# A spatial gate that leaves PSUM in its first two vector operations, with its product and its low half on GpSimd

## The chip, the cores and the metric

The kernel runs on one core of a Trainium2 chip. The metric is the device time of one execution in microseconds (us), as the median of several runs. The core has a matrix engine (PE, TensorE, with its weight loads shown apart as PEld), a vector engine (DVE, VectorE), a scalar engine (ACT, ScalarE), GpSimd (POOL) and a queue engine that issues transfers (SP). PE writes its results to PSUM; everything else lies in SBUF.

## The reference, cut to what matters

The model is a decayed linear attention, a feed-forward block and a gated block, for 4 batches of 768 tokens with 384 features. The change touches the two last lines of the gated block alone.

```python
def _moe2_ref(x, w_in, g_ln, w_sg, b_sg, w_out):
    h = gelu_tanh(x @ w_in)                       # 384 -> 1024
    u, v = h[..., :512], h[..., 512:]
    v_n = layer_norm(v) * g_ln
    v_s = np.einsum('ts,bsd->btd', w_sg, v_n) + b_sg[None, :, None]   # over the 768 tokens
    gated = u * v_s
    return x + gated @ w_out
```

## The kernel before

The tokens are cut into 24 chunks of 128 (4 batches of 6). A chunk's attention needs DMA transposes, two scans on VectorE, and small matmuls (`sc` L436, `psd` L518, `psy` L544 and L551), and it ends in an rms scale that GpSimd works out in a chain of small operations (L241 to L246). Its result `x` then goes through the feed-forward block, two chunks at a time: `pg` L633 is the first product, evicted by ScalarE (hT, L638) and VectorE (hT, L639); L667 is the second. The gated block makes `vg` from `pgv` (L707) and the factor u, called `uT`, from `pgu` (L732). Every fp32 operand of a matmul is split into two half-precision parts, a high part (a copy to f16) and a low part (the value less that copy), and each product is three matmuls. The helper `low` (L150) makes low parts, on VectorE or GpSimd.

The **spatial gate** is `D_units` (L740 to L769). It runs once per batch, when all six chunks of the batch have their `vn`. It has six units, one for each of three blocks of 256 tokens (`th`) and two halves of the features (`dp`). One unit is 36 matmuls of 128x256 into one PSUM tile `pgs`, two VectorE operations (scale by g, add b; L759), a VectorE product with u (L762), a ScalarE copy to the high part (L763), the low part (L150 through `low`) and a ScalarE square with a running sum for a range check (L766, tile `junk`, sum into `st_g`). `KG_` is 0, so `in_psum` is always true: all of these work in place in the PSUM tile `pgs`, and the low part is made on VectorE. The last reader of the tile is L766. The high and low parts overwrite the memory of `uT` (the tile `gt` is the same bytes), and so they are called `uT` in the traces. `E_units` then makes `pgo` (L781) from them, adds x on VectorE (L783), and writes the output by DMA.

PSUM tiles with tag "g" have three buffers, and `pg`, `pg2`, `pgv`, `pgu`, `pgs` and `pgo` take turns in them. PE can start a unit when the tile three units earlier has lost its last reader.

The order of the work is not written out engine by engine. Each attention step and each unit gets a due time from a table of constants (L920 to L974, `events`), the list is sorted by it, and a scheduler sets each engine's instructions in a row by its own timeline. Each engine takes its instructions in that order, and one that waits holds those behind it. The attention of later batches runs among the units of earlier ones, up to the third gate. The fourth gate has no attention beside it.

At the end of `split_path` eleven range checks (L977 to L998) are made, each of three small VectorE operations through a tile `ok` in the pool `p1` (one buffer, tag "tm"), then two more (L1000, L1001), a GpSimd all-reduce (L1002) and a cast (L1003). The program reads the flag before it ends.

Of the kernel before, what the change touches and what calls it, by code (L numbers as in the profile page):

```python
# [7 lines left out]
F32 = mybir.dt.float32  # L8
# [5 lines left out]
ALU = mybir.AluOpType  # L14
# [3 lines left out]
P = 128  # L18
EPS = 1e-6
LATE, TC, D0, DS, DX, KQ, NE, KA, LD, S0, A0, S1, A1, S2, A2, S3, A3, S4, A4, S5, A5, C0, R0, C1, R1, C2, R2, C3, R3, MB, MD, QB, HB, KV, KG_, KW, KW2 = 16.42, 19.13, 24, 0.88, 1.18, 8.0, 4.0, 8.0, 5.66, 0.8, 16, 13, 12, 28, 14, 38, 14, 46, 14, 54, 14, 2, 3, 18, 3, 36, 3, 60, 5, 224.0, 96.0, 0.0, 96.0, 19.0, 0.0, 10.0, 0.0  # L20
# [19 lines left out]
def kernel(tc, q, k, v, alpha, g1, w1, w2, w_in, g2, w_sg, b_sg, w_out, out):  # L40
    nc = tc.nc
    with ExitStack() as ctx:
        keep = ctx.enter_context(tc.tile_pool(name="keep", bufs=1))
        ident = keep.tile([P, P], F32, name="ident")
        bad = keep.tile([1, 1], I32, name="bad")
        with ExitStack() as fast:
            split_path(fast, tc, ident, bad, q, k, v, alpha, g1, w1, w2, w_in, g2, w_sg, b_sg, w_out, out)
        flag = nc.values_load(bad[0:1, 0:1], min_val=0, max_val=1)
        with tc.If(flag > 0):
            with ExitStack() as slow:  # L50
                general_path(slow, tc, ident, q, k, v, alpha, g1, w1, w2, w_in, g2, w_sg, b_sg, w_out, out)


def split_path(ctx, tc, ident, bad, q, k, v, alpha, g1, w1, w2, w_in, g2, w_sg, b_sg, w_out, out):


    nc = tc.nc
# [11 lines left out]
    U = 256  # L69
# [8 lines left out]
    p1 = ctx.enter_context(tc.tile_pool(name="p1", bufs=1))  # L78
    p2 = ctx.enter_context(tc.tile_pool(name="p2", bufs=2))
# [31 lines left out]
    def junk():  # L111
        return p2.tile([P, 512], BF16, tag="cv", name="junk")
# [36 lines left out]
    def low(on_dve, out, in0, in1):  # L149
        (nc.vector if on_dve else nc.gpsimd).tensor_tensor(out=out, in0=in0, in1=in1, op=ALU.subtract)  # L150
# [464 lines left out]
    hT, x2T, uf, uT, vn, gt = {}, {}, {}, {}, {}, {}  # L615
# [124 lines left out]
    def D_units(b):  # L740
        units = []
        for th in range(S // U):
            for dp in range(KG // 2):
                def unit(th=th, dp=dp):
                    key = (b, th)

                    gt[key] = uf[key].bitcast(F16).rearrange("p (g a f t) -> p g a f t", g=KG // 2, a=2, f=2)
                    pg = ps.tile([P, 2, U], F32, tag="g", bufs=3, name="pgs")
                    for f in range(2):
                        d = 2 * dp + f  # L750
                        for n_, (s, a, r) in enumerate([(s, a, r) for s in range(NCH) for a, r in passes]):
                            nc.tensor.matmul(out=pg[:, f, :], lhsT=vn[b * NCH + s][:, a, d * P:(d + 1) * P],  # L752
                                             rhs=wgs[th][:, r, s, :], start=(n_ == 0),
                                             stop=(n_ == 3 * NCH - 1))
                    in_psum = b >= KG_
                    tm = pg if in_psum else p1.tile([P, 2, U], F32, tag="tm", name="tm")
                    for f in range(2):
                        d = 2 * dp + f
                        nc.vector.scalar_tensor_tensor(out=tm[:, f, :], in0=pg[:, f, :], scalar=g2c[:, d:d + 1],  # L759
                                                       in1=bbc[:, th * U:(th + 1) * U], op0=ALU.mult, op1=ALU.add)  # L760
                    o = slice(2 * dp, 2 * dp + 2)
                    nc.vector.tensor_tensor(out=tm, in0=tm, in1=uT[key][:, o, :], op=ALU.mult)  # L762
                    nc.scalar.activation(out=gt[key][:, dp, 0], in_=tm, func=AF.Copy)  # L763
                    low(in_psum, gt[key][:, dp, 1], tm, gt[key][:, dp, 0])
                    n_ = b * 6 + 2 * th + dp
                    nc.scalar.activation(out=junk()[:, 0:512].rearrange("p (a b) -> p a b", a=2), in_=tm,  # L766
                                         func=AF.Square, accum_out=st_g[:, n_:n_ + 1])
                units.append((unit, 36 * U / 2400.0, NW[3]))
        return units  # L769
# [48 lines left out]
    if True:  # L818
# [2 lines left out]
            nc.gpsimd.memset(t[:, 3, :, D:64], 1.0)  # L821
        nc.vector.memset(one, 1.0)

        cols = p1.tile([P, 2 * U], F32, tag="tm", name="cols")[:, 0:P]
        ones = p2.tile([P, DG], F32, tag="vg", name="ones")[0:1, 0:P]
        nc.vector.memset(ones, 1.0)
        unit = one.to_broadcast([P, P])
# [103 lines left out]
        for j in range(NG):  # L931
            b, c, n = groups[j]
# [57 lines left out]
        verdict = big.tile([P, len(checks) + 2], F32, name="verdict")  # L990
        fails, worst, allbad = verdict[:, 2:], verdict[:, 0:1], verdict[:, 1:2]
        for n, (src, lo, hi, shape) in enumerate(checks):
            ok = p1.tile([P, 2 * U], F32, tag="tm", name="ok")
            ok = ok[:, 0:shape[0]] if len(shape) == 1 else \
                ok[:, 0:shape[0] * shape[1]].rearrange("p (a b) -> p a b", b=shape[1])
            nc.vector.tensor_scalar(out=ok, in0=src, scalar1=lo, scalar2=None, op0=ALU.is_ge)
            nc.vector.scalar_tensor_tensor(out=ok, in0=src, scalar=hi, in1=ok, op0=ALU.is_le, op1=ALU.mult)
            nc.vector.tensor_reduce(out=fails[:, n:n + 1], in_=ok, op=ALU.min,  # L998
                                    axis=AX.XY if len(shape) == 2 else AX.X)
# [242 lines left out]
```

## Time and profile before

| What | Value |
|---|---|
| median of 3 runs | 701.03 us (700.08 to 703.02) |
| the profiled execution, its own time | 702.77 us |
| span of its trace | 701.0 us |
| mean granted TensorE clock | 0.992 of full speed |
| PE busy | 650.6 us (93%) |
| DVE busy | 465.3 us (66%) |
| ACT busy | 435.5 us (62%) |
| POOL busy | 181.0 us (26%) |

The profiled execution lies 1.74 us above the median, and 1.77 us of its time lie outside the span. PE is busy for all but 50.4 us. The gates run in about 223 to 251 us (batch 0), 382 to 407 us (batch 1), 541 to 569 us (batch 2) and 660 to 683.5 us (batch 3). Shares of the whole span say little here: the other engines are far from full on average and full in places.

### The profile page before, as it was taken

What the parts mean: (1) busy time and instruction counts of PE and PEld (TensorE: products, weight loads), DVE (VectorE), ACT (ScalarE), POOL (GpSimd) and SP (SyncE); (2) the same over time, 40 slices, a digit from 0 to 9 for tenths busy, and PEclk for the clock granted to TensorE, in tenths of its full rate; (3) what the DMA queues carried; (4) which work ended last, traced back from release to release, by engine and by line L of the source; (5) the groups of instructions that cost most, each with busy time, mean ns of one, the idle gap of its engine ahead of it and who ended that gap; (6) DMA issues with size and microseconds to landing.
All of it is one profiled execution on the core that took longest, in us unless ns stands there. A gap on an engine that the chain in (4) does not pass through costs nothing.

```text
span 701.0 us, 14486 instructions
## 1 busy us (share of the span) xinstructions
PE 650.6 (93%) x5658; PEld 489.4 (70%) x5658; DVE 465.3 (66%) x911; ACT 435.5 (62%) x871; POOL 181.0 (26%) x413
## 2 busy tenths in 40 slices
PE   5889998979999988989999978998989989999996
PEld 3757776767776875667777866676656877676783
DVE  7999675867476795557745896559655678333464
ACT  5887646676878488488755688488652656322230
POOL 2121101423516220433532220432404311201100
PEclk9999999999999999999999999999999999999999
DMA  9996679765475149367382159275140612110102
GB/s 227 226 260 167 204 178 169 155 113 95 91 121 80 28 86 190 84 108 116 59 115 56 30 100 183 76 127 85 40 86 15 88 34 58 34 24 12 36 1 72
DMA packets 228637, 70.64 MB, mean 101 GB/s; under 512 B 219472, under 2 KB 222544, under 8 KB 228560
## 3 DMA queue, kind: packets, MB, share of 16 engines
q1 hardware_dynamic: 228560, 69.63, 52.0%
q8 instruction: 46, 0.75, 0.5%
q14 instruction: 31, 0.25, 0.1%
HBM read 35.79 MB, written 4.72 MB: 58 GB/s over the span
## 4 chain that ended last, share of the span: by engine, by line
PE 43%; DVE 17%; ACT 17%; DMA 13%; issue 5%; POOL 3%; SPq 1%; ACTq 0%; DVEq 0%; POOLq 0%
PE pg L667 13%; PE pg L633 9%; PE pgs L752 6%; DMA stage<-stage 4%; PE pgu L732 4%; PE pgv L707 4%; PE pgo L781 3%; ACT stage L306 3%; DMA wgs<-wsp 2%; ACT junk L500 2%; ACT stage L290 2%; DMA inp<-in_alpha_dram 2%; DVE F L345 2%; DVE sc L449 2%; DMA inp<-in_q_dram 2%
## 5 line engine op out<-in xcount | busy, mean ns | idle before, releaser
L633 PE MATMUL pg<-xhT,w1s 128*128 128x256 f16 (+1 forms) x1404 | 151.5, 267 | 13.2 <-DVE hT L639 6.1
L633 PEld LDWEIGHTS <-w1s 128*128 128x128 f16 x1404 | 128.4, 99 | 31.2 <-issue 14.9
L667 PE MATMUL pg<-w2s,hT 128*128 128x384 f16 x864 | 143.7, 326 | 0.3 <-ACT vg L710 0.3
L667 PEld LDWEIGHTS <-hT 128*128 128x128 f16 x864 | 83.9, 98 | 54.3 <-issue 0.2
L752 PE MATMUL pgs<-wgs,vn 128*128 128x256 f16 x864 | 96.1, 273 | 1.5 <-ACT junk L766 1.5
L752 PEld LDWEIGHTS <-vn 128*128 128x128 f16 x864 | 84.0, 98 | 12.0 <-issue 1.7
L639 DVE SCALAR_TENSOR_TENSOR hT<-pg,hT 128x512 f16<-128x512 f32 (+1 forms) x74 | 49.3, 672 | 46.8 <-ACT hT L638 46.6
L306 ACT ACTIVATE stage<-stage 128x1024 uint16<-128x1024 uint16 x48 | 64.7, 1354 | 19.1 <-DMA stage<-stage 19.0
L290 ACT ACTIVATE stage<-inp 128x1024 uint16<-128x1024 uint16 x48 | 50.1, 1053 | 30.3 <-DVE K L345 18.4
L150 POOL TENSOR_TENSOR kh<-K,kh 128x512 f16<-128x512 f32 x17 | 20.4, 1199 | 129.2 <-ACT kh L414 129.2
L732 PE MATMUL pgu<-x2T,wis 128*128 128x256 f16 x432 | 50.7, 274 | 1.6 <-DVE hT L639 1.3
L707 PE MATMUL pgv<-wis,x2T 128*128 128x512 f16 x216 | 49.9, 381 | 1.5 <-DVE hT L639 1.2
L781 PE MATMUL pgo<-wos,uT 128*128 128x384 f16 x288 | 48.3, 326 | 1.2 <-DVE x L783 1.2
L732 PEld LDWEIGHTS <-wis 128*128 128x128 f16 x432 | 41.7, 98 | 9.1 <-DVE hT L639 2.2
L638 ACT ACTIVATE hT<-pg 128x512 f16<-128x512 f32 (+1 forms) x74 | 42.0, 577 | 9.7 <-PE pg L633 9.6
L500 ACT ACTIVATE junk<-inp 128x384 bf16<-128x384 f32 x72 | 37.2, 519 | 8.0 <-DMA inp<-in_q_dram 4.0
L781 PEld LDWEIGHTS <-uT 128*128 128x128 f16 x288 | 28.0, 98 | 19.9 <-issue 2.0
L150 POOL TENSOR_TENSOR qs<-F,qs 128x512 f16<-128x512 f32 x18 | 20.6, 1143 | 79.7 <-ACT qs L386 79.7
L707 PEld LDWEIGHTS <-x2T 128*128 128x128 f16 x216 | 20.9, 99 | 24.4 <-issue 2.1
L468 ACT ACTIVATE ss<-sc 128x512 f16<-128x512 f32 x36 | 21.1, 596 | 19.0 <-DVE sc L449 19.0
L759 DVE SCALAR_TENSOR_TENSOR pgs<-pgs,g2c,bbc 128x256 f32<-128x256 f32 x48 | 23.4, 487 | 11.3 <-PE pgs L752 10.6
L716 DVE TENSOR_SCALAR vg<-vg,mvv,rv 128x512 f32<-128x512 f32 x24 | 13.8, 579 | 24.4 <-POOL rv L246 23.9
(172 smaller groups left out, 1100.8 us busy)
## 6 DMA issues: line engine op xcount, KB each, us to landing
stage<-in_moe_w_ch_dram SPq DMA_DIRECT2D x24, 384.0 KB, 5.2
inp<-in_alpha_dram SPq DMA_DIRECT2D x24, 192.0 KB, 3.3
inp<-in_q_dram SPq DMA_DIRECT2D x24, 192.0 KB, 4.1
inp<-in_k_dram SPq DMA_DIRECT2D x24, 192.0 KB, 4.4
inp<-in_v_dram SPq DMA_DIRECT2D x24, 192.0 KB, 4.4
out_dram<-x SPq DMA_DIRECT2D x24, 192.0 KB, 2.4
stage<-in_moe_w_in_dram SPq DMA_DIRECT2D x4, 768.0 KB, 4.3
stage<-in_moe_w_sg_dram SPq DMA_DIRECT2D x6, 384.0 KB, 3.4
```

The source lines that it names most:

```text
L150: (nc.vector if on_dve else nc.gpsimd).tensor_tensor(out=out, in0=in0, in1=in1, op=ALU.subtract)
L290: nc.scalar.activation(out=sp, in_=t[:, n].rearrange("p h d -> p (h d)").bitcast(U16) .rearrange("p (x w) -> p w x", w=2), func=AF.Copy)
L306: nc.scalar.activation(out=words[:, :, :, gap:], in_=tr, func=AF.Copy)
L500: nc.scalar.activation(out=junk()[:, 0:DM].rearrange("p (h d) -> p h d", h=H), in_=t[:, n, :, 0:D], func=AF.Square, accum_out=st_in[:, i, ...
L633: nc.tensor.matmul(out=pg[:, f, :], lhsT=w1s[:, a, kk, ff * P:(ff + 1) * P], rhs=xhT[j][:, r, kk, o], start=(n_ == 0), stop=(n_ == 3 * KD ...
L638: nc.scalar.activation(out=hi, in_=src, func=AF.Relu)
L639: last_dve[0] = nc.vector.scalar_tensor_tensor(out=lo, in0=src, scalar=0.0, in1=hi, op0=ALU.max, op1=ALU.subtract)
L667: nc.tensor.matmul(out=box[s], lhsT=hidden(a, f, s), rhs=w2s[:, r, f, :], start=(f == 0 and a == 0 and r == 0), stop=(f == KF - 1 and r == 1))
L707: nc.tensor.matmul(out=pg, lhsT=x2T[j][:, a, kk, o], rhs=wis[:, r, kk, DG:DI], start=(n_ == 0), stop=(n_ == 3 * KD - 1))
L732: nc.tensor.matmul(out=pg[:, f, :], lhsT=wis[:, a, kk, ff * P:(ff + 1) * P], rhs=x2T[j][:, r, kk, 0:N], start=(n_ == 0), stop=(n_ == 3 * K ...
L752: nc.tensor.matmul(out=pg[:, f, :], lhsT=vn[b * NCH + s][:, a, d * P:(d + 1) * P], rhs=wgs[th][:, r, s, :], start=(n_ == 0), stop=(n_ == 3 ...
L781: nc.tensor.matmul(out=pg, lhsT=gt[key][:, d // 2, a, d % 2, o], rhs=wos[:, r, d, :], start=(d == 0 and a == 0 and r == 0), stop=(d == KG ...
```

## The change

The gate's first two VectorE operations now write to a new SBUF tile `tm` (pool `p2`, two buffers) instead of back to PSUM. The product with u reads and writes `tm`, and it runs on GpSimd. The low part runs on GpSimd too. ScalarE's copy and square read `tm`. The scratch tiles `cols` (in the prologue) and `ok` (the range checks at the end) move from `p1` to `p2` with the same tag "tm", so that they take turns in the two buffers of the gate's `tm`. Line numbers after the gate fall by one.

```diff
-                    in_psum = b >= KG_
-                    tm = pg if in_psum else p1.tile([P, 2, U], F32, tag="tm", name="tm")
+                    tm = p2.tile([P, 2, U], F32, tag="tm", name="tm")
                     for f in range(2):
                         d = 2 * dp + f
                         nc.vector.scalar_tensor_tensor(out=tm[:, f, :], in0=pg[:, f, :], scalar=g2c[:, d:d + 1],
                                                        in1=bbc[:, th * U:(th + 1) * U], op0=ALU.mult, op1=ALU.add)
                     o = slice(2 * dp, 2 * dp + 2)
-                    nc.vector.tensor_tensor(out=tm, in0=tm, in1=uT[key][:, o, :], op=ALU.mult)
+                    nc.gpsimd.tensor_tensor(out=tm, in0=tm, in1=uT[key][:, o, :], op=ALU.mult)
                     nc.scalar.activation(out=gt[key][:, dp, 0], in_=tm, func=AF.Copy)
-                    low(in_psum, gt[key][:, dp, 1], tm, gt[key][:, dp, 0])
+                    nc.gpsimd.tensor_tensor(out=gt[key][:, dp, 1], in0=tm, in1=gt[key][:, dp, 0], op=ALU.subtract)
...
-        cols = p1.tile([P, 2 * U], F32, tag="tm", name="cols")[:, 0:P]
+        cols = p2.tile([P, 2 * U], F32, tag="tm", name="cols")[:, 0:P]
...
-            ok = p1.tile([P, 2 * U], F32, tag="tm", name="ok")
+            ok = p2.tile([P, 2 * U], F32, tag="tm", name="ok")
```

Since a scheduler sets the order, other instructions move as well. The first place is VectorE in the middle of the first gate, around the scans of a chunk's attention (L345 makes its running products F and K, L311 multiplies them by the staged q and k, L150 with `ss` is a low part of the scores). Before:

```order
L449 TENSOR_TENSOR sc<-sc,causal 128x512 x2
L345 SCALAR_TENSOR_TENSOR F<-stage,reset 128x516
L345 SCALAR_TENSOR_TENSOR K<-stage,reset 128x516
L150 TENSOR_TENSOR uT<-pgs,uT 128x512
L150 TENSOR_TENSOR ss_3145<-sc,ss_3145 128x512
L370 TENSOR_SCALAR st_fe<-F 128x4
L150 TENSOR_TENSOR ss_3146<-sc,ss_3146 128x512
L311 TENSOR_TENSOR K<-stage,K 128x4x128
L373 RECIPROCAL rf<-st_fe 128x4
L311 TENSOR_TENSOR F<-stage,F 128x4x128
L759 SCALAR_TENSOR_TENSOR pgs<-pgs,g2c,bbc 128x256 x2
L762 TENSOR_TENSOR pgs<-pgs,uT 128x512
```

The same place in the changed kernel:

```order
L449 TENSOR_TENSOR sc<-sc,causal 128x512 x2
L345 SCALAR_TENSOR_TENSOR F<-stage,reset 128x516
L345 SCALAR_TENSOR_TENSOR K<-stage,reset 128x516
L370 TENSOR_SCALAR st_fe<-F 128x4
L150 TENSOR_TENSOR ss_3149<-sc,ss_3149 128x512
L311 TENSOR_TENSOR K<-stage,K 128x4x128
L373 RECIPROCAL rf<-st_fe 128x4
L311 TENSOR_TENSOR F<-stage,F 128x4x128
L150 TENSOR_TENSOR ss_3150<-sc,ss_3150 128x512
L758 SCALAR_TENSOR_TENSOR tm<-pgs,g2c,bbc 128x256 x2
```

The gate's product and low part are gone from VectorE, and one low part of the scores moved behind L311. The second place is GpSimd a little later in the same gate, around the chunk's `qs`, `sp` and `state` (low part of q, low part and update of the running state) and the rms chain. Before:

```order
L150 TENSOR_TENSOR qs<-F,qs 128x512
L573 TENSOR_TENSOR sp<-state,sp 128x384
L241 TENSOR_SCALAR ve<-st_mv 128x1
L559 TENSOR_TENSOR state<-state,st_fe 128x384
L242 TENSOR_TENSOR rr<-ve,consts 128x1
L243 TENSOR_TENSOR ra<-rr,ve 128x1
L244 TENSOR_TENSOR ra<-ra,rr 128x1
```

In the changed kernel:

```order
L761 TENSOR_TENSOR tm<-tm,uT 128x512
L150 TENSOR_TENSOR qs<-F,qs 128x512
L573 TENSOR_TENSOR sp<-state,sp 128x384
L241 TENSOR_SCALAR ve<-st_mv 128x1
L763 TENSOR_TENSOR uT<-tm,uT 128x512
L559 TENSOR_TENSOR state<-state,st_fe 128x384
L242 TENSOR_TENSOR rr<-ve,consts 128x1
L761 TENSOR_TENSOR tm<-tm,uT 128x512
L243 TENSOR_TENSOR ra<-rr,ve 128x1
L244 TENSOR_TENSOR ra<-ra,rr 128x1
```

The gate's products (L761) and low parts (L763) now stand between the operations of the attention. The third place is the end of the program on VectorE. Before, it reads as follows behind the last product of the gate; the first three of the eleven checks stand far ahead of it, among the units before the fourth gate, and others follow them:

```order
L762 TENSOR_TENSOR pgs<-pgs,uT 128x512
L783 SCALAR_TENSOR_TENSOR x<-pgo,x 128x384
L150 TENSOR_TENSOR uT<-pgs,uT 128x512
L783 SCALAR_TENSOR_TENSOR x<-pgo,x 128x384
L996 TENSOR_SCALAR ok<-st_g 128x24
L997 SCALAR_TENSOR_TENSOR ok<-st_g,ok 128x24
L998 TENSOR_REDUCE verdict<-ok 128x1
```

In the changed kernel the last operations of the gate are followed by all eleven checks, from the first one on:

```order
L758 SCALAR_TENSOR_TENSOR tm<-pgs,g2c,bbc 128x256 x12
L995 TENSOR_SCALAR ok<-st_in 128x72
L996 SCALAR_TENSOR_TENSOR ok<-st_in,ok 128x72
L997 TENSOR_REDUCE verdict<-ok 128x1
L995 TENSOR_SCALAR ok<-st_in 128x24
L996 SCALAR_TENSOR_TENSOR ok<-st_in,ok 128x24
L782 SCALAR_TENSOR_TENSOR x<-pgo,x 128x384
L997 TENSOR_REDUCE verdict<-ok 128x1
```

Behind these come 27 more operations of the checks with two of L782 among them, then L999, a fourth L782, L1000, the cast L1002 and the last two of L782. The second tile `ok` takes the buffer of the gate's last `tm`.

## Rows read from the trace of the kernel before

**Rows 1.** Page, part 1: engine, busy us, share, instructions.

```profile
PE 650.6 (93%) x5658; PEld 489.4 (70%) x5658; DVE 465.3 (66%) x911; ACT 435.5 (62%) x871; POOL 181.0 (26%) x413
```

**Rows 2.** PE's waits: who waits, the releaser, total us, times, mean us.

```profile
PE pg L633 <- ACT junk L766: 5.4, 4, 1.9
...
PE pgs L752 <- ACT junk L766: 1.5, 1, 1.5
```

**Rows 3.** Busy us of engines by stretch; length first, then PE, PEld, DVE, ACT, POOL.

```profile
250.80:268.80 18.00, 14.92 (x166) 12.70 (x163) 14.96 (x29) 18.00 (x44) 3.50 (x8) 1.00 0.63 121
...
406.60:430.00 23.40, 19.01 (x173) 14.96 (x169) 17.26 (x32) 22.99 (x51) 3.71 (x10) 1.00 0.73 129
...
569.00:588.00 19.00, 15.82 (x187) 13.76 (x185) 18.11 (x34) 13.96 (x37) 4.62 (x9) 1.00 0.19 36
660.00:683.50 23.50, 23.50 (x217) 21.04 (x215) 12.83 (x22) 7.63 (x17) 0.17 (x1) 1.00 0.01 1
```

**Rows 4.** PE's timeline: start, length, instruction, idle before it and releaser.

```profile
255.51 2.13 PE L633 MATMUL pg<-xhT,w1s 128*128 128x256 f16 x18 [0.88 <-ACT junk L766]
...
259.45 4.21 PE L633 MATMUL pg<-xhT,w1s 128*128 128x256 f16 x36 [1.30 <-ACT junk L766]
```

**Rows 5.** PE's timeline at the third gate.

```profile
560.25 4.09 PE L752 MATMUL pgs<-wgs,vn 128*128 128x256 f16 x36 [1.48 <-ACT junk L766]
...
573.72 0.25 PE L551 MATMUL psy<-vs,ss 128*128 128x48 f16 x3 [1.25 <-DVE ss L150]
...
577.93 2.12 PE L633 MATMUL pg<-xhT,w1s 128*128 128x256 f16 x18 [0.89 <-DVE hT L639]
```

**Rows 6.** DVE's timeline around the scans of the first gate.

```profile
247.24 0.16 DVE L370 TENSOR_SCALAR st_fe<-F 128x4 f32<-128x4 f32 x1
247.31 0.68 DVE L150 TENSOR_TENSOR ss<-sc,ss 128x512 f16<-128x512 f32 x1
```

**Rows 7.** Groups of instructions, shapes apart: count, busy us, mean ns.

```profile
L759 DVE SCALAR_TENSOR_TENSOR pgs<-pgs,g2c,bbc 128x256 f32<-128x256 f32 x48 | 23.4, 487 | 11.3 <-PE pgs L752 10.6
L150 POOL TENSOR_TENSOR vn<-vg,vn 128x512 f16<-128x512 f32 x19 | 23.1, 1213 | 6.8 <-ACT vn L719 6.7
L762 DVE TENSOR_TENSOR pgs<-pgs,uT 128x512 f32<-128x512 f32 x24 | 16.8, 698 | 0.7
L150 DVE TENSOR_TENSOR uT<-pgs,uT 128x512 f16<-128x512 f32 x24 | 16.4, 684 | 12.2 <-ACT uT L763 12.1
...
L763 ACT ACTIVATE uT<-pgs 128x512 f16<-128x512 f32 x24 | 14.2, 590 | 21.6 <-DVE pgs L762 21.6
```

**Rows 8.** POOL's timeline in the attention after the first gate.

```profile
254.14 1.12 POOL L150 TENSOR_TENSOR qs<-F,qs 128x512 f16<-128x512 f32 x1 [3.49 <-ACT qs L386]
255.22 0.91 POOL L573 TENSOR_TENSOR sp<-state,sp 128x384 f16<-128x384 f32 x1
```

**Rows 9.** Line L147: duration ns min/median/max, first and last start.

```profile
L147 DVE SCALAR_TENSOR_TENSOR vs<-inp,vs x18: 544/764/1444, 137.6 to 580.5; 128x384 f16<-128x384 f32 x18
```

**Rows 10.** DVE's timeline at the same moment.

```profile
255.52 1.03 DVE L147 SCALAR_TENSOR_TENSOR vs<-inp,vs 128x384 f16<-128x384 f32 x1
```

**Rows 11.** DVE's timeline at the end of the program.

```profile
683.56 1.02 DVE L759 SCALAR_TENSOR_TENSOR pgs<-pgs,g2c,bbc 128x256 f32<-128x256 f32 x2 [0.82 <-PE pgs L752]
...
687.93 0.17 DVE L996 TENSOR_SCALAR ok<-st_g 128x24 f32<-128x24 f32 x1
688.13 0.18 DVE L997 SCALAR_TENSOR_TENSOR ok<-st_g,ok 128x24 f32<-128x24 f32 x1
...
692.21 0.15 DVE L1001 TENSOR_SCALAR verdict<-verdict 128x1 f32<-128x1 f32 x1
692.91 0.14 DVE L1003 CAST bad<-verdict 1x1 int32<-1x1 f32 x1 [0.55 <-POOL verdict L1002]
...
695.26 0.56 DVE L783 SCALAR_TENSOR_TENSOR x<-pgo,x 128x384 f32<-128x384 f32 x1 [1.39 <-PE pgo L781]
```

**Rows 12.** The chain of waits that ended last, its end: start, us, what.

```profile
659.94 23.58 PE pgs L752 x216
```

## The prediction

> **What bounds the kernel now.** I read the busy times first. PE works for 650.6 us of a span of 701.0 us [rows 1], so all that better flow can give is 50.4 us. Then I read PE's waits for those that the edited lines cause. Two rows name the gate's ScalarE square (L766), the last reader of the PSUM tile: 5.4 us in front of L633 and 1.5 us in front of the next gate unit [rows 2]. That is 6.9 us that the change is aimed at.
>
> The stretches tell whether such a wait can go away, or only change its name. In the first gate's end ScalarE is busy for 18.00 of 18.00 us and PE for 14.92; in the second gate's end ScalarE is busy for 22.99 of 23.40 and PE for 19.01. In the third gate's end VectorE is the full one, 18.11 of 19.00, with PE at 15.82. In the fourth gate PE works for 23.50 of 23.50 us [rows 3]. So there are three kinds of place: ScalarE bounds, VectorE bounds, PE bounds. The chain of waits agrees for the last: 216 gate matmuls in 23.58 us without a break [rows 12], 3.93 us for a unit.
>
> **First gate: the earlier release.** PE waits for L766 twice here, 0.88 and 1.30 us [rows 4]. The change frees the PSUM tile after two VectorE operations of 0.487 us [rows 7], so both of these waits end. But the next thing that PE fills is `pg`, which ScalarE and VectorE have to empty, and ScalarE has no free time in the stretch [rows 3]. It still makes the same copy and the same square for each unit, now from SBUF. PE would run two tiles ahead and wait for `hT` instead. A gain can come only if ScalarE enters the stretch earlier. VectorE's order around the scans loses one product (0.698), one low part (0.684) [rows 7] and one `ss` of 0.68 [rows 6], so K and F are ready up to 2.06 us sooner. I take half of that, **-1.0 us**, since GpSimd's rms chain now has one L761 and one L763 in it. One of these costs 1.12 to 1.21 us by the nearest rows, GpSimd's `qs` low part [rows 8] and its mean for `vn` [rows 7], so the chain may be 2.4 us later. The bounds are all of PE's idle time there, 18.00 - 14.92 = 3.1 us gained, and 2.4 lost.
>
> **Second gate.** The same case, with 23.40 - 19.01 = 4.4 us of idle PE [rows 3], and with PE's order changed: scores of the next chunk come ahead of the units that follow. ScalarE has 0.4 us free. I take half of the idle time, **-2.2 us**, with bounds of -4.4 and +2.4, again for GpSimd in the rms chain.
>
> **Third gate: VectorE relieved.** PE loses 1.48 us to L766, and 1.25 and 0.89 us to VectorE's `ss` and `hT` [rows 5]. The stretch from 569 to 588 is VectorE's. The work of the gate's last two units that falls there or just ahead of it loses 2 x (0.698 + 0.684) = 2.76 us [rows 7]. ScalarE is free for 5.0 us of the 19 [rows 3], so this should pass through: **-2.8 us**. The upper bound of the gain is 1.48 + 19.00 - 15.82 = 4.7 us. The lower is the 1.48 us alone less what a slow eviction costs. The STT that now writes SBUF is not in the trace; its nearest rows are 0.487 for 256 columns in PSUM [rows 7] and 0.56 for 384 columns from PSUM into `x` [rows 11], so it costs between 0.37 (in proportion to columns) and 0.56, and I take 0.487 as the same operation and size. Four of them make at most 0.3 us either way.
>
> **Fourth gate.** PE is full, and nothing that ends a unit earlier can speed it up: **0**. The cover is the tile rotation. A unit's chain through `tm` is 2 x 0.487 + 1.21 + 0.59 + 1.21 = 4.0 us [rows 7], and with two buffers it has 2 x 3.93 = 7.9 us. Where attention runs beside it, a `qs` and an `sp` in front cost another 2.0 us, still under 7.9. But GpSimd also stands still for 3.49 us in front of `qs`, waiting for ScalarE [rows 8]; with that in front of a product the chain is 9.5 us, and the first operations of a later unit wait for `tm`, with PE behind them.
>
> **GpSimd's and VectorE's traffic.** GpSimd gets 48 operations, 54 to 58 us. The `vs` operation of L147, which reads two SBUF tiles, takes 0.544 us at best and 1.444 at worst [rows 9]; at 255.52 it took 1.03 while GpSimd ran `sp` from 255.22 to 256.13 [rows 8, 10]. The difference is 0.49 us. I count six such operations for a chunk (two scans, two of L311, two of L147) and 1.5 chunks in a gate: nine. In the third stretch four new GpSimd operations fill 4.8 of 19 us, a quarter: 9 x 0.25 x 0.49 = **+1.1 us**. In the ScalarE-bound gates VectorE has 3 to 6 us free [rows 3], which hides it. The bounds are 0, and all nine in all three gates at 14.5 us of GpSimd in 23.58, 61%: 9 x 0.61 x 0.49 x 3 = 8.1 us.
>
> A rule speaks against the move. The Trainium skill, "GPSIMD Engine Reference", section 4.1 "Engine selection", puts elementwise work on VectorE and calls GpSimd about two times slower for two inputs (1.96 in section 3.1). The trace has 1.213 against 0.684, a ratio of 1.77, for low parts of one size [rows 7]. By the page a product would take an estimated 1.37 us, the tail's start below would be 0.3 us later, and the sum would end at 697.4.
>
> **The end of the program.** Before, the checks' operations stand early or among the last matmuls; the last `x` starts at 695.26, just behind PE, and ends at 695.82 [rows 11]. Now all eleven follow the gate. The first takes the older `tm`; the second needs the last one, which is free when the last unit's chain is over. That begins at 683.56, its two STTs end at 684.58, and 1.21 + 0.59 + 1.21 later it is 687.6. VectorE waits there with the first `x` behind it. From then on 31 small operations, four of L782 at 0.56, 0.70 from L1000 to the cast, 0.14 for it and two more of L782 stand in the row. Small ones that depend on each other start every 0.20 us [rows 11], unrelated ones as little as 0.07 us apart [rows 6], and most are now interleaved in pairs. At 0.20: 687.6 + 6.2 + 2.2 + 0.7 + 0.1 + 1.1 = 697.9. At 0.10: 694.8, which is ahead of PE, so that 695.82 stays. The bounds are 0 and +2.1, and I take the middle, **+1.0 us**.
>
> **Sum.** -1.0 - 2.2 - 2.8 + 0 + 1.1 + 1.0 = -3.9 us. The profiled execution took 702.77, of which 701.0 are span; it becomes 698.9. It lay 1.74 above the median, so the forecast is **697.1 us** against 701.03. A measurement of this kernel can tell about 0.5%, 3.5 us, from no change.
>
> **The rivals.** *Waits only move.* At the first two gates ScalarE stays full, and its late `hT` takes the place of L766; the scores moved ahead make no difference. Then -2.8 + 1.1 + 1.0 = -0.7, and the time is 700.3. For it: 18.00 of 18.00. Against it: ScalarE's queue was itself held by late K and F.
>
> *Shared traffic.* If GpSimd's operations slow VectorE in all three gates, the first two gates gain nothing, the third gains 2.8, and 8.1 + 1.0 are lost: +6.3, **707.3 us**. It decides from 1.8 us of slowing on, and is visible from 5.3 on. For it: L147's spread [rows 9]. Against it: half of the nine lie where VectorE has room. The Trainium skill, "GPSIMD Engine Reference", section 8 "Key points", says that GpSimd shares its SBUF interfaces with VectorE, and names instructions with two SBUF inputs. The slow `vs` beside `sp` agrees; the 0.49 us is the trace's.
>
> *PE's stalls all go.* If attention as a whole is early, all idle time of the three ends goes: 3.1 + 4.4 + 4.7 = 12.2, less 2.1 for traffic and tail: -10.1, 690.9 us. Against it: ScalarE's full rows.
>
> *The change does not do what it says.* If the scheduler gave `tm` too late and PE's waits named the new operations (L758 for want of `tm`), the freed time would be lost again; the time is that of the first rival, and I count it there.
>
> **How the numbers follow.** The forecast has 0.45, waits only move 0.22, shared traffic 0.15, all stalls gone 0.18. The forecast's own span is 694 to 700 (its gate terms half a bound up or down); some 0.28 of its 0.45 lies below 697.5, the rest is within 0.5%. With all stalls gone, faster is 0.46; the same is 0.17 + 0.22 = 0.39; slower 0.15. The range for 8 in 10 takes in most of the two middle cases and part of both ends: 691.0 to 703.0.
>
> **What would show it.** PE's waits for the gate's square (L765 in the changed kernel) must be gone; if its time stands at `hT` in the first two gates, the first rival holds. VectorE's rows of L147, L311 and L345 in the gates should have means not more than 0.2 us longer. ScalarE should start `kh` (L414) earlier at the first gate. In the third gate the waits for `ss` and `hT` should shrink. At the end the last `x` should end 12.3 to 14.4 us after the last gate matmul. The prediction is wrong if PE waits for gate tiles with GpSimd behind them, if GpSimd's operations take much over 1.2 us, or if attention's due order moved more than I read from the rows.

## The result, and the profile after

The changed kernel takes 697.43 us (median of 8 runs, 695.62 to 701.35), the kernel before on the same chip 702.9 us. The ratio is 0.9932, with a 95% interval of 0.991 to 0.9954: faster by 0.7%. The forecast was 697.1 us against 701.03, a ratio of 0.9944. So the sum came out, and the places did not. The first thing to read is the page's first part, and PE's waits (who waits, the releaser, total us, times, longest us), which answer [rows 1, 2]. The last number of a wait is the longest one in [rows 2] too, not the mean.

```profile
PE 650.6 (94%) x5658; PEld 490.4 (71%) x5658; DVE 437.6 (63%) x863; ACT 435.6 (63%) x871; POOL 244.9 (35%) x461
```

```profile
PE pg L633 <- DVE hT L639: 5.3, 5, 2.3
PE psy L551 <- ACT ss L468: 5.0, 2, 2.9
PE pgo L780 <- DVE hT L639: 3.6, 4, 2.0
PE psy L551 <- DVE ss L150: 2.1, 2, 1.6
```

PE's work is the same 650.6 us and the span is 695.3 for 701.0. VectorE lost 27.7 us and GpSimd got 63.9. No wait for the gate's square is left (6.9 us before). Waits for `hT` and for scores (`ss`) hold PE now.

To see where the 5.7 us of span went, I cut both traces at the same matmuls: the last one of a gate, the last `pgu` of the group behind it, and so on. Two traces of each kernel, the second ones from runs told of below. The lengths are in us.

| Stretch | before | again | changed | again |
|---|---|---|---|---|
| gate 1, 2 and 4 themselves, each | 26.3 or 23.5 | same | same | same |
| behind gate 1 | 41.20 | 41.68 | 41.16 | 41.14 |
| next group (to its 18th `pgv`) | 35.23 | 35.00 | 33.18 | 33.17 |
| from there to gate 2 | 52.46 | 52.46 | 52.53 | 52.43 |
| behind gate 2 | 43.15 | 42.54 | 44.22 | 44.03 |
| next group | 42.12 | 41.92 | 37.06 | 36.72 |
| to the end of gate 3's first matmul | 51.13 | 50.06 | 48.03 | 49.62 |
| gate 3 | 27.94 | 27.92 | 26.30 | 26.29 |
| behind gate 3 | 35.75 | 35.71 | 40.16 | 39.50 |
| rest, to the last matmul | 90.00 | 90.00 | 90.00 | 90.00 |

Not in the table are the part up to gate 1 (223.7, 224.4, 224.1 and 225.3 us) and the end behind the last matmul (5.8, 5.6, 5.9 and 6.4 us). With them the spans are 701.0 and 699.9 us before, 695.3 and 697.1 us after, so the second pair differs by 2.7 us only. All but one of the lengths in the table come again within 1.1 us; the stretch before gate 3 varies by 1.6 us. Most of the gain lies in the groups that follow a gate by some 40 us, and behind the third gate 4 us are lost.

Behind the first gate the waits of [rows 4] are gone, and PE waits for `hT` in their place. PE's timeline there (start, length, instruction, idle before it and releaser), the two other waits of the kernel before first, then the changed kernel:

```profile
264.54 4.09 PE L633 MATMUL pg<-xhT,w1s 128*128 128x256 f16 x36 [0.87 <-DVE hT L639]
...
275.68 5.52 PE L781 MATMUL pgo<-wos,uT 128*128 128x384 f16 x33 [1.01 <-DVE x L783]
```

```profile
251.87 6.06 PE L633 MATMUL pg<-xhT,w1s 128*128 128x256 f16 x54
...
260.43 2.13 PE L633 MATMUL pg<-xhT,w1s 128*128 128x256 f16 x18 [1.05 <-DVE hT L639]
...
263.35 4.40 PE L633 MATMUL pg<-xhT,w1s 128*128 128x256 f16 x36 [0.54 <-DVE hT L639]
...
269.72 2.11 PE L780 MATMUL pgo<-wos,uT 128*128 128x384 f16 x12 [1.96 <-DVE hT L639]
```

The stretches behind the second gate show what moved. Of the kernel before, then of the changed kernel (length, then busy us and instructions of PE, PEld, DVE, ACT and POOL, then the granted clock):

```profile
404.90:448.00 43.10, 37.24 (x352) 27.27 (x350) 30.75 (x54) 33.29 (x71) 10.60 (x27) 1.00 0.79 145
448.00:490.10 42.10, 38.96 (x364) 28.40 (x363) 30.63 (x52) 32.72 (x60) 13.24 (x23) 1.00 0.53 88
490.10:541.30 51.20, 48.00 (x374) 33.34 (x373) 30.47 (x55) 25.62 (x49) 17.79 (x45) 0.97 0.26 49
569.20:605.00 35.80, 32.62 (x325) 24.86 (x323) 28.26 (x57) 19.25 (x49) 8.15 (x24) 1.00 0.19 47
```

```profile
403.30:447.50 44.20, 39.66 (x374) 29.14 (x372) 32.42 (x58) 40.21 (x82) 18.23 (x28) 0.96 0.86 154
447.50:484.60 37.10, 36.48 (x343) 27.07 (x342) 25.45 (x45) 25.65 (x48) 13.02 (x26) 1.00 0.54 86
484.60:532.60 48.00, 46.51 (x373) 32.59 (x371) 30.13 (x55) 25.61 (x49) 17.80 (x45) 1.00 0.27 52
558.90:599.10 40.20, 35.24 (x325) 26.22 (x324) 26.83 (x44) 19.82 (x51) 16.30 (x29) 0.92 0.19 42
```

Some 20 matmuls and 7 us of ScalarE's work, attention of the next chunk, came from the second stretch into the first, where engines had stood idle. PE's idle time in the two together fell from 5.86 + 3.14 = 9.0 to 4.54 + 0.62 = 5.2 us. That is the scheduler's new row, not a shorter wait at the gate; two kernels below, with gate and row exchanged, bear this out.

The last row is the loss. PE's 325 matmuls are the same, but PE stands idle for 4.96 us instead of 3.18, and works for 35.24 instead of 32.62, at a granted clock of 0.92. What happened reads from four engines' timelines at the third gate:

```profile
558.91 2.19 POOL L763 TENSOR_TENSOR uT<-tm,uT 128x512 f16<-128x512 f32 x1 [0.74 <-ACT uT L762]
561.07 2.18 POOL L761 TENSOR_TENSOR tm<-tm,uT 128x512 f32<-128x512 f32 x1
```

```profile
558.93 1.22 DVE L345 TENSOR_TENSOR_SCAN F<-stage,reset 128x516 f32<-128x516 f32 x1
560.07 2.12 DVE L345 TENSOR_TENSOR_SCAN K<-stage,reset 128x516 f32<-128x516 f32 x1
562.12 1.16 DVE L370 TENSOR_SCALAR st_fe<-F 128x4 f32<-128x4 f32 x1
```

```profile
563.28 0.63 ACT L762 ACTIVATE uT<-tm 128x512 f16<-128x512 f32 x1 [3.83 <-POOL tm L761]
...
564.43 1.06 ACT L468 ACTIVATE ss<-sc 128x512 f16<-128x512 f32 x2
```

```profile
565.06 0.22 PE L551 MATMUL psy<-vs,ss 128*128 128x48 f16 x1 [2.88 <-ACT ss L468]
565.79 0.30 PE L551 MATMUL psy<-vs,ss 128*128 128x48 f16 x3 [0.51 <-DVE ss L150]
567.65 0.98 PE L551 MATMUL psy<-vs,ss 128*128 128x48 f16 x20 [1.56 <-DVE ss L150]
568.46 7.70 PE L633 MATMUL pg<-xhT,w1s 128*128 128x256 f16 x54
```

GpSimd's low part and product meet VectorE's two scans. Each of the two on GpSimd takes 2.2 us, and the second scan takes 2.12. ScalarE's copy waits 3.83 us for the product, with the scores' copies (L468) behind it in the row, and PE waits 2.88 + 0.51 + 1.56 us for those. Then the next 54 matmuls take 7.70 us; the same number took 6.06 behind the first gate, where the clock was not lowered. At their start the granted clock is 0.50, the lower of its two levels (1.2 GHz), after that idle time:

```profile
568.40:570.50 2.10, 2.10 (x16) 1.54 (x14) 1.08 (x3) 2.10 (x7) 1.31 (x2) 0.50 0.57 106
```

### The profile page after: what moved, and what is told of

Read it like the earlier page. It is cut to its first block, busy times and chain, and to the rows that moved or that the text cites. A ratio compares the mean times of both kernels' runs of the same rounds, so it can differ in the third digit from the quotient of the medians.

```text
span 695.3 us, 14515 instructions
## 1 busy us (share of the span) xinstructions
PE 650.6 (94%) x5658; PEld 490.4 (71%) x5658; DVE 437.6 (63%) x863; ACT 435.6 (63%) x871; POOL 244.9 (35%) x461
## 4 chain that ended last, share of the span: by engine, by line
PE 48%; ACT 17%; DMA 13%; DVE 12%; POOL 5%; issue 4%; SPq 1%; ACTq 0%; DVEq 0%; POOLq 0%
PE pg L667 13%; PE pg L633 9%; PE pgs L752 6%; PE pgo L780 5%; PE pgu L732 4%; DMA stage<-stage 4%; PE pgv L707 4%; DMA wgs<-wsp 2%; ACT stage L306 2%; ACT junk L500 2%; ACT stage L290 2%; DMA stage<-in_moe_w_ch_dram 2%; PE pw L141 2%; ACT hT L638 2%; DMA inp<-in_q_dram 2%
## 5 line engine op out<-in xcount | busy, mean ns | idle before, releaser
L638 ACT ACTIVATE hT<-pg 128x512 f16<-128x512 f32 (+1 forms) x74 | 41.9, 572 | 12.6 <-PE pg L633 12.4
L150 POOL TENSOR_TENSOR kh<-K,kh 128x512 f16<-128x512 f32 x17 | 21.3, 1250 | 74.1 <-ACT kh L414 73.3
L758 DVE SCALAR_TENSOR_TENSOR tm<-pgs,g2c,bbc 128x256 f32<-128x256 f32 x48 | 20.9, 477 | 40.4 <-PE pgs L752 30.8
L150 POOL TENSOR_TENSOR qs<-F,qs 128x512 f16<-128x512 f32 x18 | 20.5, 1139 | 60.3 <-ACT qs L386 60.1
L761 POOL TENSOR_TENSOR tm<-tm,uT 128x512 f32<-128x512 f32 x24 | 32.4, 1348 | 18.4 <-DVE tm L758 18.3
L762 ACT ACTIVATE uT<-tm 128x512 f16<-128x512 f32 x24 | 14.9, 622 | 37.1 <-POOL tm L761 37.1
```

What stands on the lines that cost most here:

```text
L638: nc.scalar.activation(out=hi, in_=src, func=AF.Relu)
```

## Experiments

Two questions were open: is it the early release or VectorE's relief that gains, and how much of it is the row in which the scheduler sets the instructions. All ratios are to the kernel before on the same chip.

**Release without relief.** Both operations back on VectorE, in `tm`:

```diff
-nc.gpsimd.tensor_tensor(out=tm, in0=tm, in1=uT[key][:, o, :], op=ALU.mult)
+nc.vector.tensor_tensor(out=tm, in0=tm, in1=uT[key][:, o, :], op=ALU.mult)
-nc.gpsimd.tensor_tensor(out=gt[key][:, dp, 1], in0=tm, ...
+nc.vector.tensor_tensor(out=gt[key][:, dp, 1], in0=tm, ...
```

> The changed kernel, but with the product with u and the low part back on VectorE, working in the SBUF tile tm: only the early release of the PSUM tile is left of the change. If the release alone makes the gain, the waits of PE for the gate's square stay away and the time stays near the changed kernel's, some 697 us (ratio to before 0.990 to 0.995). If relieving VectorE of 33 us makes the gain, it is lost: 700 to 702 us (ratio 0.998 to 1.002). If traffic shared between GpSimd and VectorE costs the changed kernel several us, this one is the faster, under 695 us.

Measured: 697.31 us, 0.9915 (0.99 to 0.9929). VectorE's relief isn't needed for the gain. (The trace kept of this kernel is of its slowest run, 700.46 us.)

**Relief with a later release.** The square reads the PSUM tile:

```diff
-in_=tm, func=AF.Square, accum_out=...
+in_=pg, func=AF.Square, scale=2.0 ** -16, accum_out=...
```

> The changed kernel, but the square for the range check reads the PSUM tile pgs, scaled by 2^-16, instead of tm (it leaves the factor u out of that check's sum): the PSUM tile is held until ScalarE's last operation, VectorE stays relieved. If the early release is the gain, PE's waits for the square (4 to 7 us) make 700 to 704 us (ratio 0.997 to 1.003). If relieved VectorE or another row of attention is the gain, part of it stays: 697.5 to 699.5 us (ratio 0.993 to 0.996).

Measured: 698.27 us, 0.9931 (0.9912 to 0.995), although PE waits for the square again, 4.0 us in four places. This is not relief without release, as it was meant to be: the square no longer has to wait for the product, and ScalarE makes it ahead of the copy. From a unit's last matmul to the end of the tile's last reader it is 8.2 us in the kernel before, 4.5 in this one and 2.7 in the changed one (means of the first three gates). So the release needn't be as early as in the changed kernel; whether relief gains without any earlier release is not shown. A first form without the scale put the check's sum out of its bound, and the program went on into its general path (4798 us); it tells nothing here.

Early release without relief gives the whole gain, and relief adds nothing to it that can be seen. That doesn't fit a sum of both. What these kernels have in common is that the tile is free sooner, and that the scheduler places attention otherwise.

**The row held.** For three of the next four kernels I recorded the place of each of the 7681 instructions in its engine's row and tied each to the one in front of it, for issue order only (`how` is a dependency of the class NoSync). Where gate and row come from different kernels, the gate's product and low part are left free, and 7633 instructions are tied.

```diff
+for step in row:
+    at += step
+    if last is not None:
+        tc.add_manual_dep(traced[at], traced[last].name, how, reason="row")
+    last = at
```

The purest case first: the kernel before, its row kept whole, but VectorE's product writes SBUF and so frees the PSUM tile (and `ok` has a tile of its own):

```diff
-tm = pg if in_psum else ...
+tm = p2.tile([P, 2, U], F32, tag="tm", name="tm")
...
-nc.vector.scalar_tensor_tensor(out=tm[:, f, :], in0=pg[:, f, :], ...
+nc.vector.scalar_tensor_tensor(out=pg[:, f, :], in0=pg[:, f, :], ...
...
-nc.vector.tensor_tensor(out=tm, in0=tm, in1=uT[key][:, o, :], op=ALU.mult)
+nc.vector.tensor_tensor(out=tm, in0=pg, in1=uT[key][:, o, :], op=ALU.mult)
```

> The kernel before with one thing changed: the product with u writes the SBUF tile tm, which ScalarE and the low part read, so the PSUM tile is free after three VectorE operations. Every instruction of every engine stands in the row of the kernel before (the range checks keep a scratch tile of their own), and GpSimd gets nothing. If the early release as such makes the gain, PE's waits for the square go and the time is 695 to 698 us (ratio 0.989 to 0.993). If it is the scheduler's other row that the release allows, the waits go but the time stays within 0.4% of the kernel before: 700 to 703 us (ratio 0.996 to 1.000).

Measured: 703.02 us, 1.001 (0.9999 to 1.0022). PE's waits in this kernel:

```profile
PE pg L633 <- DVE hT L639: 8.6, 5, 2.5
PE psy L551 <- DVE ss L150: 6.4, 8, 3.0
```

The 6.9 us of waits for the square are all gone, `hT` went from 6.1 to 8.6 us and `ss` from 4.5 to 6.4, and nothing is gained. The stretch behind gate 3 is 2.3 us longer than before. In the trace all four engines' operations come in the order of the kernel before. That kernel with its row merely held was not run, so a price of the holding itself is not excluded.

The same gate, with the row that the scheduler makes for it:

> Both first operations stay in PSUM, VectorE's product with u writes the SBUF tile tm, and the low part is VectorE's from tm: the PSUM tile is free after three VectorE operations, some 1.7 us, and GpSimd gets nothing. If early release is what matters, this gains like the changed kernel or a little more, as with both operations on VectorE: 696 to 698 us (ratio 0.990 to 0.994). If VectorE's relief matters, 700 us and more.

Measured: 696.06 us, 0.9903 (0.9883 to 0.9924). Between these two only the row, its holding and the checks' scratch tile differ, and together they are worth 1.1%.

The changed kernel's gate in the row of the kernel before:

> The changed kernel's gate (SBUF tile, product and low part on GpSimd) with every other instruction of every engine in the row in which the kernel before has it; the range checks keep a scratch tile of their own so that this row can be kept. If the gain comes from the gate's data path (earlier release, VectorE relieved), it stays: some 697 us (ratio 0.990 to 0.995). If it comes from the other row in which the scheduler put the attention, above all behind the second gate, most of it is lost: 700 to 702.5 us (ratio 0.996 to 1.000).

Measured: 700.06 us, 0.9974 (0.995 to 0.9998): by the medians little more than a third of the gain is left; the interval allows almost none, or three quarters. Behind the first gate its stretch is 44.7 us, 3.5 longer than before.

The gate of before in the changed kernel's row:

> The gate of the kernel before (all in PSUM, product and low part on VectorE) with every other instruction of every engine in the row in which the changed kernel has it. If the row makes the gain, the time is 697 to 699 us (ratio 0.992 to 0.995) although PE waits for the gate's square again. If the data path makes it, the time is at 700 to 706 us (ratio 0.997 to 1.005), with 5 to 9 us of PE waiting for the square.

Measured: 713.88 us, 1.0148 (1.0124 to 1.0172), and PE's waits:

```profile
PE pg L633 <- ACT junk L765: 14.3, 5, 4.4
...
PE pgs L752 <- ACT junk L765: 3.4, 1, 3.4
```

Both expectations were missed. So the new row alone is not the gain either: with the old gate it makes PE wait 17.7 us for the square.

The last two kernels also show which of the two shortens the second group after gate 2, the largest single gain. It takes 42.12 us before and 37.06 in the changed kernel; with the new gate in the old row it takes 41.9, and with the old gate in the new row 37.9. That gain is the row's. With the old gate the same row loses more than that in front of it, 50.3 us behind gate 2 for 43.15.

The row is not the whole of the differences, though; a part is TensorE's clock. From the end of the first gate's first matmul to the end of the stretch behind gate 3, with the same matmuls in all, in us:

| Kernel (one trace each) | length | PE works | PE idle |
|---|---|---|---|
| before; again | 381.6; 379.9 | 357.5; 355.9 | 24.1; 24.0 |
| changed; again | 375.2; 375.5 | 358.3; 358.4 | 16.9; 17.0 |
| early release, row of before | 380.6 | 359.3 | 21.3 |
| early release, its own row | 373.5 | 355.7 | 17.8 |
| new gate, row of before | 377.4 | 359.1 | 18.3 |
| old gate, row of the changed | 393.9 | 365.7 | 28.1 |

Where PE works longer, the granted clock was lower for a while: with the new gate in the old row it is 0.92 in the stretch behind gate 1, and PE works 40.29 us there for 37.10 before. In idle time the early release saves 2.8 us in the old row and 6.3 in its own, and the new gate keeps 5.8 of its 7.2 us in the old row; there PE's longer work takes 1.6 to 3.4 us of this back. So the early release gains in time only with a row that uses it, and some of what the old row loses is lost to the clock.

**The third gate's loss.** VectorE's first operations wait 8.9 us for a free `tm`, held by GpSimd's low part. Four buffers for `tm`, shared with `vg`:

```diff
-tm = p2.tile([P, 2, U], F32, tag="tm", name="tm")
+tm = p2.tile([P, 2, U], F32, tag="vg", bufs=4, name="tm")
```

> The changed kernel, but tm shares one ring of four buffers with vg (the same SBUF as two rings of two), so that in a gate up to four tiles tm can be under way. If the third gate's loss comes from VectorE's waits for a tm tile (8.9 us in front of L758, with the scores queued behind), these waits go, and the time falls by 2 to 4 us against the changed kernel, to some 694 us (ratio 0.987 to 0.990). If the loss comes from GpSimd's operations stretched beside the scans (2.2 us for 1.2), it stays near 697 us.

Measured: 698.44 us, 0.9944 (0.9926 to 0.9961), no better. The wait for GpSimd's low part is gone from VectorE's list, and the stretch behind gate 3 is still 39.95 us. PE, ScalarE and GpSimd have the row of the changed kernel, VectorE too up to the checks at the end. So that wait cost nothing. The product moved back to VectorE, the low part left on GpSimd:

```diff
-nc.gpsimd.tensor_tensor(out=tm, in0=tm, in1=uT[key][:, o, :], op=ALU.mult)
+nc.vector.tensor_tensor(out=tm, in0=tm, in1=uT[key][:, o, :], op=ALU.mult)
```

> The changed kernel with the product with u back on VectorE, in the SBUF tile tm; the low part stays on GpSimd. GpSimd's chain in a unit is shorter by some 1.3 us, and VectorE has 16.8 us more, with two SBUF inputs. If the tm tiles' long life costs the changed kernel time at the third gate, this one gains 1 to 3 us there and is at 694 to 696 us (ratio 0.988 to 0.992). If relief of VectorE makes the gain, half of the 5 us is lost: some 699.5 us (ratio 0.996).

Measured: 698.87 us, 0.995 (0.9933 to 0.9966). Behind gate 3 the stretch is 33.5 us, 6.6 shorter than in the changed kernel, but behind gate 1 it is 1.3 longer and the next group after gate 2 is 3.9 longer. The row changed there too. The time is near the 699.5 us that was expected if VectorE's relief makes the gain, but the kernel without any relief, at 0.9915, speaks against that reading. The same with both first operations in PSUM:

```diff
-out=tm[:, f, :], in0=pg[:, f, :], scalar=g2c[:, d:d + 1], ...
+out=pg[:, f, :], in0=pg[:, f, :], scalar=g2c[:, d:d + 1], ...
-nc.gpsimd.tensor_tensor(out=tm, in0=tm, in1=uT[key][:, o, :], op=ALU.mult)
+nc.vector.tensor_tensor(out=tm, in0=pg, in1=uT[key][:, o, :], op=ALU.mult)
```

> Both first operations in PSUM, VectorE's product with u writes tm, the low part is GpSimd's: half of the new GpSimd work, none of it in front of ScalarE's copy. If GpSimd's low parts are free beside VectorE, VectorE's 16 us of relief show in a ratio of 0.986 to 0.989, better than with all work on VectorE (0.990). If they stretch the scans and stand in the rms chain, it is 0.991 to 0.995, no better than the changed kernel.

Measured: 698.95 us, 0.9949 (0.9935 to 0.9964), at the edge of the second range; behind gate 3 it is 33.5 us again. GpSimd's product is out of ScalarE's way in both, and the third gate's loss is gone in both. That fits the timeline above, though the rows differ too, so it is not shown apart from them. And two kernels with product and low part on GpSimd don't have the loss either: 34.3 us with the new gate in the old row, 35.9 where the square reads the PSUM tile. So GpSimd's operations cost this time only as the changed kernel's row places them beside the scans.

**The two kernels again.**

> The kernel before once more, unchanged, for a second trace: how much the stretches between the gates differ from execution to execution. If the 2.5 us wait and the 5 us shorter stretches between the second and third gate belong to the kernel and not to one execution, the lengths of the first trace come again within 1 us: 41.2, 35.2, 43.2, 42.1, 51.1 and 35.8 us. If they are chance, some of them are off by 2 us or more.

> The changed kernel once more, on the same chip as the runs beside it. Its ratio should come again at 0.991 to 0.995. A variant whose interval lies under it is better than the change; if it is 0.990 itself, the variants without GpSimd are no better. Its trace should show the first trace's stretches again within 1 us (41.2, 33.2, 44.2, 37.1, 48.0 and 40.2 us).

Measured: 701.66 us for the kernel before (one run), and 697.57 us, 0.9919 (0.9906 to 0.9931), for the changed one. The lengths are in the table above; in both kernels the one up to gate 3 misses its 1 us (by 1.07 and 1.59). The 2.5 us wait of the kernel before came again, as 2.60 us. No variant is clear of this interval on the fast side; the product that evicts, without GpSimd, has the lowest ratio (0.9903), and the two intervals overlap.

## Why the prediction was right, and where not

The forecast of -3.9 us and a ratio of 0.9944 stands against -5.5 us, 0.9932 and 0.9919. That 697.1 us so nearly meets 697.43 is in part luck: the kernel before took 702.9 us beside the changed one, not the 701.03 that the forecast started from. The terms do worse than their sum.

- **First gate, -1.0.** Measured 0 (-0.04, and -0.54 in the second pair). The step that failed is that K and F would be ready up to 2.06 us sooner and that half of it would reach PE. ScalarE's `kh` (L414), which waits for K, starts 24.11 us after the end of the gate's first matmul, for 24.96: 0.85 us sooner. The K scan took 2.13 us for 1.21 there, beside GpSimd's new work. On VectorE, before and then changed:

```profile
244.93 1.21 DVE L345 TENSOR_TENSOR_SCAN K<-stage,reset 128x516 f32<-128x516 f32 x1
```

```profile
244.82 2.13 DVE L345 TENSOR_TENSOR_SCAN K<-stage,reset 128x516 f32<-128x516 f32 x1
```

  And the 0.85 us did not reach PE. The rival *waits only move* holds here: 0.88 and 1.30 us for the square, 0.87 for `hT` and 1.01 for `x` became 1.05, 0.54, 1.96 and 0.16 for `hT`, and PE's idle time in the stretch is 3.8 us for 4.1.
- **Next group.** No term. It is 2.1 and 1.8 us shorter in the two pairs of traces; waits of 0.89 and 0.42 us for `ss` are gone there.
- **Second gate, -2.2.** The stretch behind it is 1.1 us longer, the next one 5.1 shorter: -4.0 together, and -3.7 in the second pair. The sign was right, the size too small and the place wrong. The prediction saw that scores come earlier and gave that no price of its own; its rival even said that it makes no difference. It was the largest gain.
- **Up to the third gate.** No term. 3.1 us shorter in the first pair, 0.4 in the second; part of the first was one execution's luck: a lower clock that cost the kernel before 1.4 us in its first trace and nothing in its second (last section).
- **Third gate, -2.8.** In the gate 1.6 us were gained: the 1.48 of [rows 5]. Behind it 4.4 and 3.8 us were lost, +2.8 and +2.2 in all. The step that failed is "ScalarE is free for 5.0 us of the 19 [rows 3], so this should pass through". ScalarE had time, but its copy stood in its row in front of the scores and waited for GpSimd. The prediction named GpSimd's queue and the rms chain, and not the copy that waits for GpSimd on ScalarE.
- **Fourth gate, 0.** Right. PE works without a break, and 90.0 us from there on are equal.
- **Traffic, +1.1.** The K scan went from 1.206 to 1.388 us, 16 times, 2.9 us in all, and the other operations with two SBUF inputs changed by less than 1 us each in sum. The bound held. The prediction let VectorE's free time hide the traffic in the first two gates; but the slowed scan of the first gate stands in front of the K that ScalarE waits for. GpSimd paid at the third gate. Its new operations take 61.5 us, where 54 to 58 were forecast:

```profile
L761 POOL TENSOR_TENSOR tm<-tm,uT 128x512 f32<-128x512 f32 x24 | 32.4, 1348 | 18.4 <-DVE tm L758 18.3
L763 POOL TENSOR_TENSOR uT<-tm,uT 128x512 f16<-128x512 f32 x24 | 29.1, 1212 | 17.2 <-ACT uT L762 17.2
...
L758 DVE SCALAR_TENSOR_TENSOR tm<-pgs,g2c,bbc 128x256 f32<-128x256 f32 x48 | 20.9, 477 | 40.4 <-PE pgs L752 30.8 <-POOL uT L763 8.9 <-POOL state L559 0.7
```

  The low part was forecast at 1.21 and took 1.212; the product took 1.348, 0.14 more than its bound. The operation that now writes SBUF took 0.477 (0.487 taken).
- **The end, +1.0.** Measured +0.2: from the last matmul to the end of the span 5.92 us for 5.77 (6.36 for 5.61 in the second pair). The wait that I put there did not come. The second `ok` is written at 680.46, before GpSimd's last low part has read its `tm` (680.81 to 681.96), so it had another buffer, and the sentence on that buffer in the section on the change was wrong. On VectorE, then on GpSimd:

```profile
678.87 1.29 DVE L996 SCALAR_TENSOR_TENSOR ok<-st_in,ok 128x72 f32<-128x72 f32 x1
...
680.46 0.18 DVE L995 TENSOR_SCALAR ok<-st_in 128x24 f32<-128x24 f32 x1
...
689.38 0.56 DVE L782 SCALAR_TENSOR_TENSOR x<-pgo,x 128x384 f32<-128x384 f32 x1 [0.19 <-PE pgo L780]
```

```profile
678.81 1.26 POOL L761 TENSOR_TENSOR tm<-tm,uT 128x512 f32<-128x512 f32 x1 [0.77 <-DVE tm L758]
680.81 1.15 POOL L763 TENSOR_TENSOR uT<-tm,uT 128x512 f16<-128x512 f32 x1 [0.74 <-ACT uT L762]
```

  The rest of that term was right: the pairs of small operations start 0.1 us apart, and the last `x` follows PE.

So the time was met because a gain that I put too small behind the second gate and left out elsewhere stood against a loss behind the third that I took for a gain. The reason given, that waits for the square and VectorE's relief are time, doesn't hold: the kernel that releases early in the old row gains nothing (1.001), and the one without relief gains all (0.9915). The early release gains together with the row that the scheduler makes for it, and granted clock is part of the difference. Which of the moved instructions carry the gain was not tried one by one, nor was relief without any earlier release. The prediction said that it would be wrong if attention's order moved more than was read from the rows. It did move more, and the sum was saved by the errors' signs.

The Trainium skill, "GPSIMD Engine Reference", section 4.1 "Engine selection", would have left both operations on VectorE. The runs agree in so far that GpSimd earned nothing: with both on VectorE the ratio is 0.9915, with the product that evicts 0.9903. Beside no other work a product takes 1.27 us on GpSimd at the fourth gate and 0.698 on VectorE [rows 7], a ratio of 1.8 where section 3.1 has 1.96.

## What to carry to other kernels

A wait that an edit removes is a gain only if the engine behind it is not late as well; if that engine is full in the stretch, the wait changes its name. Where a scheduler sets the rows, an edit has two effects, the data path and the other row, and they can be measured apart by holding the row; price each moved group of instructions (here some 20 matmuls into idle time), not the wait alone. Compare PE's working time as well as its idle time, since a lowered clock can take back what fewer waits give. Before work goes to a slower engine, look at who waits for its result, and at what stands behind that waiting instruction in its engine's row.

## What the runs showed of the hardware

VectorE and GpSimd seem to take turns where both read two SBUF tiles. From 558.91 to 563.28 two scans and two GpSimd operations take nearly the sum of their times alone: 1.21 + 1.21 + 1.15 + 1.27 = 4.8 us for 4.4. Even short operations are held to the other's end. At the end of the program a VectorE operation on 72 columns (L996) takes 1.29 us and ends at 680.16, where GpSimd's product ends at 680.07; the 128x4 operation at 562.12 takes 1.16 us for 0.16 [rows 6] and ends at 563.28 with GpSimd's product at 563.25. That one has a single SBUF input. The Trainium skill, "GPSIMD Engine Reference", section 1 "Specifications", tells of contention with VectorE instructions that have two SBUF inputs or run in a 2-port mode. The traces agree for two inputs, and here the wait lasts to the end of the other's operation. Whether the 128x4 operation runs in such a mode no run shows, and none measured the contention by itself.

PE's granted clock fell to 0.50 after it had stood idle for 2.88, 0.51 and 1.56 us with a few small matmuls between, and the 54 matmuls behind took 1.6 us longer than at the full clock. Behind the second gate of the changed kernel the same followed a wait of 2.26 us, and in the kernel before one of 2.53 us in the stretch up to the third gate. PE's timeline at these two places, and the stretch with the lower clock in the kernel before:

```profile
414.81 3.79 PE L633 MATMUL pg<-xhT,w1s 128*128 128x256 f16 x18 [2.26 <-DVE hT L639]
```

```profile
515.41 3.48 PE L633 MATMUL pg<-xhT,w1s 128*128 128x256 f16 x18 [2.53 <-DVE hT L639]
```

```profile
517.00:518.90 1.90, 1.90 (x10) 1.30 (x9) 0.92 (x1) 1.30 (x2) 0.00 (x0) 0.50 0.63 120
```

Where 2.1 us is usual for 18 such matmuls, these took 3.79 and 3.48. So in these three places the lower clock cost 1.4 to 1.7 us on top of the wait, which no term of the prediction had. It does not follow every such wait: in the second trace of the kernel before the same wait came at the full clock.

```profile
515.61 2.12 PE L633 MATMUL pg<-xhT,w1s 128*128 128x256 f16 x18 [2.60 <-DVE hT L639]
```
